# A hand-written operation order replaced by another in an attention-plus-MLP kernel, with fewer dummy matmuls and one more pre-summed batch

## The chip, the cores and the metric

The kernel runs on one core of one Trainium2 chip. The metric is the device time of one execution in microseconds (us), taken as the median over several executions. A difference of about 1% is what a measurement of this kernel can tell from no change.

The engines are named as in the profile: PE is the matmul engine (PEld its weight loads), DVE the vector engine, ACT the scalar engine, POOL the engine that also issues the software-driven DMAs, SP the one that issues the other DMAs. Each engine runs its own instructions strictly in the order in which the program lists them, and semaphores make it wait for the other engines.

## The reference

There are 8 batches, 8 heads, 576 tokens, head size 64. 16 "beacon" keys and values stand ahead of the 576 ordinary ones and are always visible; the others are causal. The attention output, 4608 tokens by 512, goes through a two-layer MLP (512 to 2048 to 512) with an ELU between.

```python
scores = scale * np.matmul(q, k_all.transpose(0, 1, 3, 2))   # k_all = beacon_k, k
scores = np.where(causal, -1000000000.0, scores)
a = np.exp(scores - scores.max(-1, keepdims=True))
a /= a.sum(-1, keepdims=True) + 1e-09
attn = np.matmul(a, v_all)
x = attn.transpose(0, 2, 1, 3).reshape(B * S, H * D)
h = x @ w_in
g = np.where(h > 0.0, h, np.exp(np.minimum(h, 0.0)) - 1.0)
out = g @ w_out
```

## The kernel before, in words

**An order written out by hand.** The kernel defines small steps, each a Python function of a few instructions, and then one long string (L790 to L912) lists 1501 words such as `S.3.3` or `lk.3.0`. A word is a step's name and its arguments. The helper `run` (L784) goes through the string and emits every step's instructions. So the string is at the same time the order of the instructions on each engine: PE takes its instructions from the words that have matmuls, POOL takes its own from the words that issue its DMAs, and so on. No engine overtakes within its own list.

**Attention.** Scores are made transposed, keys on partitions. Heads go in pairs p = 0 to 3. For one pair and batch the causal blocks (five key chunks j) lie behind one another as 1664 columns. From batch 1 on, the 4 x 1664 columns of a batch are cut into 13 groups of 512: `S.b.g` (L309) makes group g on PE, `x.b.g` (L330) takes the exponential on ACT, `m` (L347) masks the diagonal blocks on DVE. So group 3 holds the end of pair 0 and the start of pair 1. `L.b.g` (L402; here g is a half of the heads, pairs 2g and 2g+1) makes the row sums on PE with a matrix of ones, `n` the reciprocals on ACT, `W.b.g` (L449) the product with V, and `M.b.g` (L479) scales the result into the MLP's input. Batch 0 has a finer cut of its own.

**How q and k arrive.** Batches 0 to 2 are loaded by POOL (`lq`, L247), transposed on PE (`T`, L255) and copied to `qks` by DVE or ACT (`cq`, `ck`). Batches 3 to 7 go another way. `lk.b.n` (L758) is a POOL DMA that converts all of q (n = 0) or k (n = 1) of batch b to bf16 in DRAM, as `scr`. `lt.b.x` (L763) issues two transposing DMAs on SP, first q and then k, for the pairs 2x and 2x+1; each reads the whole half of `scr`, so `lt.b.x` needs both `lk.b.0` and `lk.b.1`, whichever x it is. They write `stq[b % 2][x]`, the staging buffer that batch b-2 used. `lp.b.x` (L773) is a small POOL step that puts the beacon keys and zeros into the same buffer; it must wait until the transposes or score matmuls of batch b-2 have read the columns that it overwrites. `lv` (L780) loads V; two V buffers go round.

**Pre-summed batches.** For batches 3 to 7, the steps `D.b.p.n` (L387) add the five key chunks of a pair's exponentials on DVE into the free buffer `qks`, and `L` then needs one pass of ones over the sum in place of one pass for each chunk.

**The MLP.** `F` (L503) is the first layer on PE, `e`, `u`, `k` or `e`, `r`, `g` the ELU on ACT and DVE (the second form puts one ACT step onto DVE). `G`, `o`, `s` are the second layer for the first token tiles. From tile 2 on, `Q` (L618) and `J` (L632) make the second layer with seven products in place of eight, from sums prepared by `Z`, `wt`; tiles 8 and 9 do the same for the first layer (`P`, `K`, `X`, `H`, `E`, `U`, `V`). A trailing `.v` on `J`, `U`, `K` puts a copy or a relu on DVE in place of ACT.

**Dummy matmuls.** `warm.4` (L204) is four matmuls of 512 columns, `wm.4` (L211) four of 128 columns, on zeros, into a bank that nobody reads. Before: three `warm.4` and eighteen `wm.4`, all ahead of the first `F`.

```python
            if b >= BD:                                   # L418, BD = 3
                for i in range(4):
                    nc.tensor.matmul(out=r_[32 * i:32 * (i + 1), QA:S], lhsT=ones, rhs=presum[b, 2 * g + i // 2] ...
            else:
                quad(b, g, QA, S, r_[:, QA:S], None, True)
        for n_ in range(2):                               # L766, lt
            nc.sync.dma_start_transpose(out=t[:, :, n_, NB:SK], in_=scr[b, n_] ...
```

Of the kernel before, what the change touches and what calls it, by code (L numbers as in the profile page):

```python
# [17 lines left out]
def kernel(  # L18
# [12 lines left out]
    P = 128  # L31

    B, H, S, D = q.shape
# [44 lines left out]
    BD = 3  # L78
# [305 lines left out]
    presum = {}  # L384
# [17 lines left out]
    def L(b, g):  # L402
# [388 lines left out]
    warm.4 warm.4 lq.0.0.0.4 lq.0.1.0.4 lv.0.2 warm.4 wm.4 ident T.0.0.0 bt ck.0.0.0 wm.4  # L791
    T.0.1.0 bk cb.0.2 cb.0.0 wm.4 lq.0.0.4.8 S.0.0.0 x.0.0.0 lq.0.1.4.8 T.0.0.1 lq.1.0.0.4 tri
    cq.0.1.0 cb.0.1 S.0.1.0 x.0.1.0 lv.0.0.1 T.0.1.1 wm.4 cq.0.0.1 S.0.0.2 x.0.0.2 S.0.0.1 wm.4
    cq.0.1.1 T.0.3.0 cb.0.3 x.0.0.1 cq.0.3.0 m.0.0.2 S.0.1.3 x.0.1.3 T.0.2.0 cq.0.2.0 S.0.1.1
    wm.4 x.0.1.1 T.0.2.1 S.0.3.0 wm.4 wm.4 x.0.3.0 T.0.3.1 cq.0.2.1 cq.0.3.1 S.0.2.0 wi.0
    S.0.2.3 x.0.2.0 wm.4 wm.4 x.0.2.3 wm.4 wm.4 m.0.0.0 m.0.2.0 m.0.1.0 S.0.3.1 x.0.3.1 wm.4
    S.0.1.2 x.0.1.2 m.0.3.0 cb.1.3 L.0.A S.0.0.3 S.0.2.1 x.0.0.3 x.0.2.1 wm.4 S.0.3.2 x.0.3.2
    T.1.0.0 n.0.A T.1.1.0 wm.4 wm.4 W.0.A.0 cb.1.0 cq.1.0.0 m.0.2.3 S.1.1 m.0.1.3 m.0.1.2
    m.0.3.2 cb.1.1 ck.1.1.0 x.1.1 wm.4 wm.4 S.1.2 W.0.A.1 x.1.2 S.0.3.3 x.0.3.3 S.0.2.2 m.0.0.3
    x.0.2.2 M.0.A.0 M.0.A.1 F.0.2 e.0.2 u.0.2 k.0.2 lv.0.3.4 S.1.5 x.1.5 m.0.2.2 S.1.0 F.0.1  # L800
    x.1.0 F.0.0 m.0.3.3 e.0.1 u.0.1 k.0.1 L.0.B n.0.B W.0.B.1 M.0.B.1 F.0.3 e.0.0 e.0.3 u.0.0
    u.0.3 W.0.B.0 S.1.4 x.1.4 wi.1 F.0.4 M.0.B.0 k.0.3 F.1.1 lq.1.0.4.8 e.0.4 u.0.4 e.1.1 k.0.0
    r.1.1 S.1.3 cb.1.2 x.1.3 g.1.1 F.0.5 T.1.3.0 cq.1.3.0 e.0.5 u.0.5 T.1.2.0 ck.1.2.0 k.0.5
    F.1.7 e.1.7 r.1.7 g.1.7 S.1.6 x.1.6 F.1.4 e.1.4 r.1.4 g.1.4 S.1.11 S.1.7 x.1.11 F.0.6 x.1.7
    S.1.8 F.1.5 k.0.4 H.1.0 e.0.6 r.0.6 x.1.8 wo.0 lq.2.0.4.8 g.0.6 G.0.1.0 e.1.5 r.1.5 g.1.5
    S.1.12 x.1.12 lq.2.0.0.4 wo.1 S.1.9 x.1.9 F.1.2 lv.1.0.1 S.1.10 x.1.10 F.1.3 m.1.2.1 cb.2.1
    wo.2 e.1.3 T.2.2.0 u.1.3 cq.2.2.0 T.2.1.0 ck.2.1.0 G.0.0.0 e.1.2 u.1.2 T.2.0.0 lv.1.2.3.4
    ck.2.0.0 lv.2.2.3.4 T.2.3.0 k.1.3 wo.3 cq.2.3.0 F.0.7 G.0.0.1 cb.2.0 e.0.7 m.1.0.0 m.1.2.0
    S.2.1 x.2.1 wt.1.0 S.2.0 m.1.1.0 G.0.1.1 F.1.0 m.1.0.1 S.2.3 lp.4.0 x.2.0 m.1.1.1 m.2.0.0
    m.1.3.1 u.0.7 L.1.0 m.1.3.0 e.1.0 r.1.0 g.1.0 x.2.3 F.1.6 n.1.0 M.1.0.0 k.0.7 L.1.1 H.1.2  # L810
    n.1.1 G.0.1.2 lk.3.0 e.1.6 u.1.6 M.1.1.0 lv.2.0.1 k.1.2 W.1.0 M.1.0.1 W.1.1 S.2.2 M.1.1.1
    x.2.2 F.2.6 cb.2.2 e.2.6 S.2.4 H.2.2 S.2.5 x.2.5 F.2.11 u.2.6 m.2.0.1 e.2.11 u.2.11 lk.3.1
    G.0.0.2 k.2.11 k.1.6 k.2.6 cb.2.3 G.0.0.3 x.2.4 F.2.8 lt.3.0 e.2.8 F.2.14 u.2.8 o.0.0 s.0.0
    S.2.8 wt.1.1 wt.2.0 e.2.14 u.2.14 S.2.12 x.2.8 k.2.14 wt.2.1 F.2.15 k.2.8 F.2.0 e.2.15
    u.2.15 G.1.1.0 e.2.0 x.2.12 G.1.1.1 r.2.0 k.2.15 g.2.0 S.2.6 x.2.6 F.2.9 G.1.1.2 S.2.11
    S.2.7 F.2.1 e.2.9 x.2.11 x.2.7 r.2.9 m.2.3.1 g.2.9 G.0.1.3 e.2.1 u.2.1 S.2.9 S.2.10 x.2.10
    F.2.2 m.2.1.0 lp.3.0 e.2.2 F.2.13 x.2.9 m.2.1.1 G.1.1.3 o.1.1 e.2.13 L.2.0 m.2.2.1 u.2.2
    r.2.13 g.2.13 S.3.3 G.1.0.0 n.2.0 M.2.0.0 x.3.3 o.0.1 F.2.3 e.2.3 u.2.3 F.2.4 S.3.1 x.3.1
    k.2.2 k.2.1 H.1.1 W.2.0 wt.4.0 M.2.0.1 e.2.4 u.2.4 m.2.3.0 lt.3.1 lp.3.1 m.2.2.0 S.3.4 s.0.1
    x.3.4 F.2.10 F.2.12 k.2.4 S.3.8 L.2.1 k.2.3 e.2.10 u.2.10 e.2.12 r.2.12 x.3.8 G.1.0.1 g.2.12  # L820
    n.2.1 k.2.10 F.2.5 e.2.5 M.2.1.0 u.2.5 F.2.7 S.3.2 x.3.2 e.2.7 W.2.1 M.2.1.1 S.3.6 Q.2.0.7
    F.3.5 wt.3.0 x.3.6 H.4.2 S.3.9 S.3.0 u.2.7 Z.2.3.0 k.2.7 Q.2.7.14 e.3.5 u.3.5 x.3.9 x.3.0
    k.2.5 Z.2.1.0 Z.2.3.1 Z.2.1.1 F.3.2 e.3.2 Z.2.2.0 F.3.8 S.3.11 e.3.8 u.3.2 k.3.2 m.3.0.0
    S.3.5 x.3.5 G.1.0.2 G.1.0.3 F.3.1 o.1.0 x.3.11 S.3.12 wt.4.1 m.3.1.0 u.3.8 S.3.10 m.3.1.1
    Q.2.14.21 e.3.1 u.3.1 k.3.1 lk.4.1 x.3.12 F.3.0 Z.2.2.1 k.3.5 m.3.0.1 J.2.0 e.3.0 Q.2.21.28
    lk.4.0 lt.4.0 D.3.0.0 D.3.1.0 u.3.0 k.3.0 D.3.1.1 s.1.0 D.3.1.2 Q.2.28.35 J.2.1 k.3.8 F.3.14
    S.4.1 x.3.10 lk.5.0 lp.4.1 Z.2.4.0 e.3.14 u.3.14 k.3.14 S.4.0 x.4.0 D.3.0.1 x.4.1 Q.2.35.42
    F.3.4 Q.2.42.49 D.3.0.2 e.3.4 u.3.4 Z.2.4.1 D.3.1.3 J.2.2.v F.3.9 e.3.9 u.3.9 Q.2.49.56
    k.3.4 S.4.4 lp.5.0 x.4.4 lv.3.0.1 S.3.7 F.3.6 k.3.9 Q.2.56.63 D.3.0.3 e.3.6 u.3.6 x.3.7
    lk.5.1 m.3.3.1 F.3.15 e.3.15 u.3.15 F.3.3 S.4.3 lv.3.2.3.4 W.3.0 lt.4.1 x.4.3 H.2.0 e.3.3  # L830
    u.3.3 m.3.2.0 lt.5.0 H.4.0 wt.3.1 k.3.15 m.3.3.0 k.3.6 L.3.0 Q.2.63.70 Q.2.70.77 k.3.3 J.2.3
    n.3.0 D.3.2.0 F.3.11 e.3.11 D.3.3.0 M.3.0.1 F.3.12 D.3.3.1 M.3.0.0 m.3.2.1 Q.2.77.84 u.3.11
    D.3.3.2 e.3.12 u.3.12 D.3.2.1 D.3.2.2 lp.5.1 Z.3.3.0 F.3.7 e.3.7 u.3.7 D.3.3.3 Q.2.84.91
    D.3.2.3 S.4.11 x.4.11 S.4.12 x.4.12 k.3.7 J.2.4 F.3.10 e.3.10 k.3.11 r.3.10 g.3.10 F.3.13
    L.3.1 n.3.1 M.3.1.0 W.3.1 Q.2.91.98 M.3.1.1 lt.5.1 k.3.12 Z.3.1.0 e.3.13 u.3.13 J.2.5 k.3.13
    m.4.3.1 F.4.8 e.4.8 S.4.10 x.4.10 S.4.2 F.4.3 x.4.2 e.4.3 u.4.8 Q.2.98.105 Q.2.105.112
    m.4.0.1 u.4.3 J.2.6.v S.4.6 S.4.5 Z.3.3.1 m.4.1.0 Q.3.0.7 x.4.5 k.4.3 x.4.6 F.4.7 e.4.7
    Q.3.7.14 u.4.7 m.4.0.0 F.4.6 S.5.4 e.4.6 u.4.6 m.4.1.1 x.5.4 S.4.7 k.4.8 Q.3.14.21 Z.3.1.1
# [102 lines left out]
```

## Time and profile before

| what | us |
|---|---|
| median of three executions | 335.81 |
| lowest, highest | 334.82, 337.05 |
| the profiled execution, device time | 336.74 |
| its span (first to last instruction) | 335.0 |
| PE busy in the span | 325.6 |
| DVE, ACT, POOL busy | 284.7, 278.1, 90.9 |

The span is 1.7 us shorter than the device time of the same execution. Busy shares are averages over the whole span; which engine a stage hangs on is read from the stage itself. A matmul row in a timeline gives the start and the modelled end; two rows behind one another overlap by some 0.1 us, so the time that a step costs PE is the distance from its start to the next start.

### The profile page before, as it was taken

The page shows a single profiled execution, that of the slowest core. Times are in us where ns is not written, and L with a number is a line of the kernel's source. Part 1 is how long each engine was busy: PE and PEld are TensorE (multiplying, and loading weights), DVE is VectorE, ACT ScalarE, POOL GpSimd, SP SyncE. Part 2 cuts the span into 40 slices and gives each one's busy share as a digit, 9 for nine tenths or more (in the row PEclk, how much of TensorE's full clock was granted, in tenths as well). Part 3 has the DMA queues.
Part 4 walks back from the last instruction along what each step waited for, and adds up shares of the span by engine and source line. Part 5 has one row for each costly group of instructions (what it writes and reads, how often), then busy time and mean ns, then how long its engine had stood idle before and what let it go on. Part 6 is the DMA issues. An engine that isn't in the chain of part 4 may idle for free.

```text
span 335.0 us, 8848 instructions
## 1 busy us (share of the span) xinstructions
PE 325.6 (97%) x3616; PEld 210.7 (63%) x3616; DVE 284.7 (85%) x601; ACT 278.1 (83%) x452; POOL 90.9 (27%) x117
## 2 busy tenths in 40 slices
PE   8899999999999999999999999999999999999994
PEld 3566766544455565656566656655666888788783
DVE  3555788875979999999899989998999999999982
ACT  2689999799999988999997998988987586889610
POOL 8968268630017284440061050000000000000000
PEclk9989999999999999999999999999999999999999
DMA  9999999999909999999199094320110110111112
GB/s 115 157 179 175 205 189 163 158 154 162 163 3 102 172 140 173 166 178 118 53 136 151 5 68 102 71 35 31 38 61 31 45 54 31 48 47 33 64 65 95
DMA packets 129113, 34.66 MB, mean 103 GB/s; under 512 B 112944, under 2 KB 127536, under 8 KB 129072
## 3 DMA queue, kind: packets, MB, share of 16 engines
q0 software_dynamic: 94944, 18.49, 68.8%
q1 hardware_dynamic: 33408, 15.34, 22.8%
q8 instruction: 28, 0.46, 0.6%
q10 hardware_dynamic: 720, 0.26, 0.3%
q14 instruction: 13, 0.11, 0.1%
HBM read 37.22 MB, written 15.34 MB: 157 GB/s over the span
## 4 chain that ended last, share of the span: by engine, by line
PE 87%; DVE 3%; ACT 3%; POOL 2%; DMA 2%; issue 1%; ACTq 0%; DVEq 0%; POOLq 0%
PE hps L512 30%; PE ops L627 29%; PE sc L321 8%; PE ut L378 6%; PE hps L697 5%; PE ops L563 4%; PE lt L378 2%; DMA kst<-in_k_dram 2%; ACT et L336 2%; POOL qst L136 1%; PE lt L420 1%; PE w L214 1%; PE tp L267 1%; PE ub L378 1%; DVE gt L554 1%
## 5 line engine op out<-in xcount | busy, mean ns | idle before, releaser
L512 PE MATMUL hps<-xT,w_in 128*128 128x512 f16 (+1 forms) x544 | 118.5, 354 | 0.3
L336 ACT ACTIVATE et<-sc 128x1024 f16<-128x1024 f32 (+2 forms) x114 | 105.7, 978 | 10.1 <-PE sc L321 9.5
L627 PEld LDWEIGHTS <-gt 128*128 128x128 f16 x768 | 73.3, 98 | 20.2 <-issue 3.7
L522 ACT ACTIVATE e<-hps 128x512 f32<-128x512 f32 x120 | 73.5, 620 | 13.8 <-PE hps L512 11.2
L512 PEld LDWEIGHTS <-w_in 128*128 128x128 f16 x544 | 50.6, 98 | 41.4 <-issue 4.4
L537 DVE SCALAR_TENSOR_TENSOR gt<-e,r 128x512 f16<-128x512 f32 x100 | 67.0, 684 | 8.0 <-ACT r L527 7.9
L527 ACT ACTIVATE r<-hps 128x512 f16<-128x512 f32 x100 | 61.9, 626 | 0.0
L627 PE MATMUL ops<-w_out,gt 128*128 128x256 f16 x384 | 50.7, 273 | 0.4 <-DVE gt L537 0.4
L627 PE MATMUL ops<-wt,gt 128*128 128x256 f16 x384 | 50.7, 273 | 0.0
L149 POOL DMA_DIRECT2D v<-in_v_dram x40 | 34.7, 919 | 5.0 <-DMA w_out<-in_moe_w_out_dram 2.7
L341 DVE TENSOR_TENSOR et<-et,triu 128x512 f16<-128x512 f16 (+4 forms) x108 | 31.2, 332 | 2.6 <-ACT et L336 2.4
L584 DVE TENSOR_TENSOR gt<-gt 128x1024 f16<-128x1024 f16 x48 | 32.4, 685 | 0.5
L378 PEld LDWEIGHTS <-v 128*32 128x32 f16 (+1 forms) x800 | 17.1, 96 | 10.6 <-issue 3.1
L394 DVE TENSOR_TENSOR qk<-qk,et 128x672 f16<-128x672 f16 (+2 forms) x60 | 21.2, 368 | 0.4
L378 PE MATMUL ut<-et,v 128*32 128x464 f16 (+3 forms) x560 | 20.9, 296 | 0.0
L472 DVE TENSOR_TENSOR xT<-ut,rl 128x672 f16<-128x672 f32 (+12 forms) x26 | 16.4, 670 | 3.1 <-PE ut L378 2.1
L643 DVE TENSOR_TENSOR osb<-ops,sm 128x512 f32<-128x512 f32 x24 | 16.4, 683 | 2.0 <-PE ops L627 1.9
L627 PE MATMUL ops<-w_out,s 128*128 128x256 f16 x128 | 17.1, 273 | 0.0
L563 PE MATMUL ops<-w_out,gt 128*128 128x512 f16 x64 | 16.0, 380 | 0.0
L736 DVE SCALAR_TENSOR_TENSOR gt<-e,r 128x512 f16<-128x512 f32 x24 | 15.9, 684 | 0.1
L627 PEld LDWEIGHTS <-s 128*128 128x128 f16 x128 | 12.3, 98 | 3.1 <-issue 0.3
L554 DVE TENSOR_TENSOR gt<-hps,r 128x512 f16<-128x512 f32 x20 | 13.7, 687 | 0.7
(111 smaller groups left out, 408.1 us busy)
## 6 DMA issues: line engine op xcount, KB each, us to landing
out_dram<-osb SPq DMA_DIRECT2D x35, 256.0 KB, 2.3
v<-in_v_dram POOLq DMA_DIRECT2D x24, 128.0 KB, 8.1
scr<-in_q_dram POOLq DMA_DIRECT2D x5, 576.0 KB, 15.6
scr<-in_k_dram POOLq DMA_DIRECT2D x5, 576.0 KB, 14.1
w_in<-in_moe_w_in_dram POOLq DMA_DIRECT2D x16, 128.0 KB, 5.9
w_out<-in_moe_w_out_dram POOLq DMA_DIRECT2D x4, 512.0 KB, 10.1
qst<-in_q_dram POOLq DMA_DIRECT2D x4, 288.0 KB, 8.7
kst<-in_k_dram POOLq DMA_DIRECT2D x4, 288.0 KB, 9.4
```

The costliest lines, as they stand in the source:

```text
L149: nc.gpsimd.dma_start(out=vt[b][r0:r0 + n, j, :, :], in_=v[b, :, ilo[j]:ilo[j] + n, :].rearrange("h s d -> s h d"),)
L321: nc.tensor.matmul(out=s[:, h, a - c0:e - c0], lhsT=t[D * h:D * (h + 1), 1, P * j:P * (j + 1)], rhs=t[D * h:D * (h + 1), 0, NB + qa + a - ...
L336: nc.scalar.activation(out=ets[b, d][:, :, a - EC2 * d:e - EC2 * d], in_=sc[b, g][:, :, a - c0:e - c0], func=AFT.Exp, bias=0.0, scale=SCALE)
L341: nc.vector.tensor_tensor(out=o, in0=o, in1=i, op=ALU.mult)
L378: nc.tensor.matmul(out=t[32 * i:32 * (i + 1), a - qa:e - qa], lhsT=ones[0:kc[j], :] if half is None else v16[0:kc[j], j, h, 32 * half:32 * ...
L512: nc.tensor.matmul(out=h[:, n_, :], lhsT=w_in16[:, cc, P * fc:P * (fc + 1)], rhs=xt[k][:, cc, a - TT * k:e - TT * k], start=(cc == 0), sto ...
L522: nc.scalar.activation(out=eb[t, i], in_=flat(hp[t, i]), func=AFT.Exp, bias=0.0, scale=1.0)
L527: nc.scalar.activation(out=rb[t, i], in_=flat(hp[t, i]), func=AFT.Relu, bias=0.0, scale=1.0)
L537: nc.vector.scalar_tensor_tensor(out=half(t, i), in0=eb[t, i], scalar=1.0, in1=rb[t, i], op0=ALU.subtract, op1=ALU.min)
L563: nc.tensor.matmul(out=ob[t, tb_], lhsT=gt[:, fc, P * tb_:P * (tb_ + 1)], rhs=w_out16[:, fc, :], start=(fc == 0), stop=(fc == NFC - 1))
L584: (nc.vector if eng == "v" else nc.gpsimd).tensor_tensor(out=o_, in0=a_, in1=b_, op=op_)
L627: nc.tensor.matmul(out=xy[t, n_][:, qd, :], lhsT=lw[:, P * qd:P * (qd + 1)], rhs=wt_[:, c, :], start=(first and qd == 0 and c == 0), stop= ...
```

## The change

Three things change; every other function stays as it is.

First, the condition in `L` is now whether a sum exists, `(b, 2 * g) in presum`, in place of `b >= BD`. Second, the string has ten `wm.4` fewer (eight are left) and eight new words `D.2.0.0` to `D.2.1.3`, so that `L.2.0` takes the pre-summed form; `L.2.1` keeps the old one. Third, the words are in another order throughout. Some choices of engine change with it: eighteen words carried `.v`, now fourteen do, and twenty ELU blocks used the DVE form, now nineteen do. In all ACT has 457 instructions for 452, DVE 597 for 594, PE 3560 matmuls for 3616; POOL and SP have the same ones in another order.

The POOL queue, from the string (each word is one to eight DMAs, or a few short POOL instructions):

- before: lq.0.0.0.4, lq.0.1.0.4, lv.0.2, ident, lq.0.0.4.8, lq.0.1.4.8, lq.1.0.0.4, tri, lv.0.0.1, wi.0, lv.0.3.4, wi.1, lq.1.0.4.8, wo.0, lq.2.0.4.8, lq.2.0.0.4, wo.1, lv.1.0.1, wo.2, lv.1.2.3.4, lv.2.2.3.4, wo.3, lp.4.0, **lk.3.0**, lv.2.0.1, **lk.3.1**, lp.3.0, lp.3.1, lk.4.1, lk.4.0, lk.5.0, lp.4.1, lp.5.0, lv.3.0.1, lk.5.1, lv.3.2.3.4, lp.5.1, lv.5, lk.6.0, lk.6.1, lv.4, ...
- after: lq.0.0.0.4, ident, lq.0.1.0.4, lq.0.0.4.8, tri, lq.0.1.4.8, lv.0.2, lv.0.0.1, lq.1.0.0.4, wi.0, lv.0.3.4, wi.1, lq.1.0.4.8, wo.0, wo.1, lp.3.0, lq.2.0.4.8, lq.2.0.0.4, wo.2, lv.1.0.1, lv.2.2.3.4, lp.4.0, lv.2.0.1, lv.1.2.3.4, lp.4.1, wo.3, **lk.3.1**, lp.3.1, **lk.3.0**, lv.3.0.1, lk.5.1, lk.7.0, lk.4.0, lk.4.1, lk.7.1, lv.3.2.3.4, lk.5.0, lk.6.1, lp.6.0, lk.6.0, lp.5.0, lp.5.1, lp.6.1, lv.4, ...

The SP queue at its start:

- before: **lt.3.0**, s.0.0, **lt.3.1**, s.0.1, lt.4.0, s.1.0, J.2.1, lt.4.1, lt.5.0, ...
- after: **lt.3.1**, **lt.3.0**, s.0.1, lt.4.0, s.1.0, J.2.1, lt.4.1, s.0.0, J.2.4, lt.5.0, ...

PE's order around the first use of batch 3 (`S.3.3`):

- before: ..., F.2.2, F.2.13, G.1.1.3, L.2.0, **S.3.3**, G.1.0.0, F.2.3, F.2.4, S.3.1, W.2.0, S.3.4, F.2.10, F.2.12, S.3.8, ...
- after: ..., F.2.2, F.2.13, L.2.0, **S.3.3**, G.0.1.3, F.2.3, G.1.0.0, F.2.4, S.3.1, W.2.0, S.3.4, F.2.12, F.2.10, G.1.0.1, S.3.8, ...

The matmul words ahead of the first `F` (F.0.2) are the same in both, apart from `wm.4`. The diff, cut:

```diff
-            if b >= BD:
+            if (b, 2 * g) in presum:
...
-    warm.4 warm.4 lq.0.0.0.4 lq.0.1.0.4 lv.0.2 warm.4 wm.4 ident T.0.0.0 bt ck.0.0.0 wm.4
-    T.0.1.0 bk cb.0.2 cb.0.0 wm.4 lq.0.0.4.8 S.0.0.0 x.0.0.0 lq.0.1.4.8 T.0.0.1 lq.1.0.0.4 tri
...
-    S.0.2.3 x.0.2.0 wm.4 wm.4 x.0.2.3 wm.4 wm.4 m.0.0.0 m.0.2.0 m.0.1.0 S.0.3.1 x.0.3.1 wm.4
...
-    n.1.1 G.0.1.2 lk.3.0 e.1.6 u.1.6 M.1.1.0 lv.2.0.1 k.1.2 W.1.0 M.1.0.1 W.1.1 S.2.2 M.1.1.1
...
-    G.0.0.2 k.2.11 k.1.6 k.2.6 cb.2.3 G.0.0.3 x.2.4 F.2.8 lt.3.0 e.2.8 F.2.14 u.2.8 o.0.0 s.0.0
...
+    lq.0.0.0.4 warm.4 warm.4 warm.4 ident bt wm.4 wm.4 T.0.1.0 wm.4 bk T.0.0.0 lq.0.1.0.4 cb.0.0
+    ck.0.1.0 cb.0.1 S.0.1.0 cq.0.0.0 S.0.0.0 lq.0.0.4.8 tri T.0.0.1 T.0.1.1 cq.0.0.1 cq.0.1.1
...
+    cb.2.2 g.0.6 x.1.8 e.1.5 r.1.5 g.1.5 cb.2.0 G.0.1.0 lp.3.0 S.1.12 x.1.12 k.0.4 S.1.9 x.1.9
...
+    u.2.11 m.2.1.0 lp.4.1 wo.3 G.0.0.2 G.0.0.3 x.2.5 F.2.8 D.2.0.0 e.2.8 F.2.14 u.2.8 H.2.2
...
+    D.2.0.1 k.2.14 D.2.0.2 e.2.15 F.2.9 u.2.15 k.2.8 G.1.1.0 D.2.1.0 S.2.8 m.2.1.1 D.2.1.1
+    lk.3.1 G.1.1.1 x.2.8 e.2.9 F.2.0 u.2.9 S.2.11 D.2.1.2 e.2.0 r.2.0 g.2.0 D.2.1.3 S.2.7
+    G.1.1.2 D.2.0.3 F.2.1 G.1.1.3 x.2.11 k.2.9 x.2.7 S.2.10 e.2.1 u.2.1 S.2.9 x.2.9 x.2.10 F.2.2
+    lp.3.1 wt.4.0 e.2.2 u.2.2 k.2.15 lk.3.0 lt.3.1 F.2.13 lt.3.0 o.1.1 e.2.13 L.2.0 S.3.3
+    G.0.1.3 n.2.0 m.2.2.0 m.2.3.0 m.2.2.1 r.2.13 g.2.13 o.0.1 F.2.3 e.2.3 M.2.0.0 k.2.1 r.2.3
...
```

## The prediction

> **What bounds the kernel now.** I read the page first, its busy line and its slices:
>
> ```profile
> PE 325.6 (97%) x3616; PEld 210.7 (63%) x3616; DVE 284.7 (85%) x601; ACT 278.1 (83%) x452; POOL 90.9 (27%) x117
> ...
> PEclk9989999999999999999999999999999999999999
> DMA  9999999999909999999199094320110110111112
> ```
>
> PE looks like the bound, the DMA engines are full for the first quarter, and in the third slice the PE clock drops. Next, the busy time by stretches, cut at the drop and where the first `F` begins:
>
> ```profile
> core 0: us, PE busy (x) PEld busy (x) DVE busy (x) ACT busy (x) POOL busy (x), PEclk, DMA share, GB/s
> 0.00:16.30 16.30, 13.26 (x180) 7.64 (x180) 6.90 (x20) 7.50 (x9) 14.58 (x28) 1.00 1.18 135
> 16.30:19.70 3.40, 3.40 (x41) 2.55 (x36) 3.03 (x15) 1.82 (x4) 1.33 (x3) 0.50 1.66 187
> 19.70:28.00 8.30, 7.20 (x183) 5.11 (x181) 4.17 (x13) 8.26 (x11) 7.02 (x12) 1.00 1.26 173
> 28.00:330.60 302.60, 301.75 (x3222) 195.38 (x3220) 270.13 (x553) 260.17 (x430) 67.95 (x76) 1.00 0.90 99
> ```
>
> From 28.0 to 330.6 us PE is busy for 301.75 of 302.60 us. Starts in its timeline are spaced alike for like work (0.22 us for a 512-column `F` matmul, 0.11 for a 256-column `Q`); I find six longer gaps in the whole stretch, 1.4 us together. So no order can gain much there, and any wait put in front of PE is paid in full. Before 28 us, ACT's timeline shows who waits:
>
> ```profile
> 8.70 4.95 ACT L336 ACTIVATE et<-sc 128x832 f16<-128x832 f32 x6 [1.13 <-PE sc L321]
> 15.49 0.86 ACT L336 ACTIVATE et<-sc 128x832 f16<-128x832 f32 x1 [1.84 <-PE sc L321]
> 16.91 1.62 ACT L336 ACTIVATE et<-sc 128x832 f16<-128x832 f32 x2 [0.55 <-PE sc L321]
> 19.55 3.89 ACT L336 ACTIVATE et<-sc 128x832 f16<-128x832 f32 x5 [1.02 <-PE sc L321]
> ```
>
> There 1.84 + 0.55 + 1.02 = 3.4 us of the exponentials' chain are lost. Last, the resource that the new order disturbs most, the transposing loads of batch 3 on SP, and PE where batch 3 is first used (the row at 83.67 is `S.3.3`):
>
> ```profile
> 62.73 7.82 SPq L767 DMA_TRANSPOSE qst<-scr  x2
> 71.71 0.38 SPq L576 DMA_DIRECT2D out_dram<-osb  x1
> 72.26 7.45 SPq L767 DMA_TRANSPOSE kst<-scr  x2
> 86.27 0.36 SPq L576 DMA_DIRECT2D out_dram<-osb  x1
> 86.84 2.74 SPq L767 DMA_TRANSPOSE qst<-scr  x2
> ```
>
> ```profile
> 82.74 0.90 PE L378 MATMUL lt<-et,ones 128*32 128x464 f16 x24
> 83.46 0.27 PE L378 MATMUL lt<-et,v 128*32 128x112 f16 x8
> 83.67 0.40 PE L321 MATMUL sc<-qst 64*128 64x48 bf16 x6
> ```
>
> The DMA view, asked for each issue alone, gives the landings. The four transposes of batch 3 start at 62.73, 69.17, 72.26 and 75.42 and land after 8.4, 7.8, 9.6 and 10.6 us: at 71.1, 77.0, 81.9 and 86.0. lt.4.0, issued at 86.84 and 88.33 as the DMA load ends, lands after 4.0 and 3.9 us, at 90.8 and 92.2. lk.3.0 lands at 62.6, lk.3.1 at 69.1. So lt.3.0 was ready 6.7 us ahead of `S.3.3`, and lt.3.1 12 us ahead of its first user at 98.4.
>
> **The change part by part.** The sum goes against the profiled execution, 336.74 us (span 335.0 and 1.7 around it), 0.9 above the median.
>
> *Dummies.* Forty fewer. At 17.16 to 18.98 sixteen of them took 1.82 us of PE, with S.0.3.1 queued behind; ACT's wait of 1.02 us ended with it. The rest stand in gaps where PE waits anyway, and cost nothing.
>
> *Start.* `F.0.2` started at 27.88, right after S.0.2.2, whose bank an exponential had to free. The same sixteen S groups, S.1.1, S.1.2 and their ACT work precede it in both orders. I lose 0.5 us at the first exponential (bk's transposes and two wm.4 now precede T.0.1.0), gain about 1.0 of the 1.84 (the loads behind T.0.2.1 have lv.0.2, 144 KB, no longer ahead of them; its two DMAs land 0.8 us apart, and its issue took 1.5) and, of the other waits, the 0.55 and the 1.02 plus 0.5 elsewhere: 2.6 us earlier. Bound on the gain: `F.0.2` needs wi.0, as deep in the POOL queue as before; its last DMA, issued at 19.81, lands after 4.9 us at 24.8, so at most 3.0. Bound on the loss: the clock row; a window at 0.50 of 3.4 us costs 1.7 us, so -1.0 to +3.0.
>
> *Pre-sum of batch 2.* L.2.0 went from 82.74 to 83.67, 0.93 us; batch 3's summed ones take 0.45. Gain 0.5. On DVE it adds 2 x (634 + 500 + 369 + 234) ns = 3.5 us of adds between 66 and 84 us, where DVE is busy 12.0 of 18.0 us; hidden. D.2.1.0 must wait for S.2.6 (its buffer), which moves 4 us forward for that; the ELU of F.2.0 queues behind it. Without that room L.2.0 would start late by up to 3.5 us.
>
> *Engine choices.* ACT gets 5 instructions more, about 3 us (0.6 each), DVE 3 more with the eight adds in it. Over 300 us this lies beside PE.
>
> *POOL order, up to V.* lp.3.0 now stands ahead of the four loads of batch 2 and must wait for the q part of T.1.2.0 (PE at 40.2, less 2.6), so these issue at 38 in place of 29.7. The queue hides most: their old landings, 40.5 to 44.9, were set by the DMAs ahead, and wo.1 (2.6 us per 512 KB between landings) now fills that time. They land near 44 to 48.4, T.2.1.0 wants the last at 48. lv.1.2.3.4 now follows lv.2 (five V loads, 0.8 us each) and lp.4.0; it lands at 54.1 + 3.7 + 1 to 2 for gaps, 59 to 60.5; W.1.0 uses it from 59.4 on. I take 1.0 us of PE waits for both; bounds 0 and 3.
>
> *lk.3 and lt.3.* Both lk.3 are issued after wo.3, lk.3.1 first. The bytes ahead of the second are the same as before and the DMA engines are full, so the second one lands at about 70: the old 69.1 and 1 for gaps (bounds 67.8, the sum of landing distances since lq.1.0.4.8 with no gap, and 72). Any lt.3 needs both, so the first transpose starts at 70, not 62.7. And SP issues lt.3.1 first, while `S.3.3` needs lt.3.0: four transposes stand ahead of `S.3.3` after 70, where one stood after 69.1. POOL's next words (lv.3.0.1, lk.5.1, lk.7.0, lk.4.0, lk.4.1, lk.7.1; three such lk kept the engines full from 62 to 87) load the same engines throughout. Under that load the first took 8.4 us and the next landings followed by 5.8, 4.9 and 4.1 us; other loaded pairs (lt.5.0, lt.6.0) by 3.4. So the fourth lands at 70 + 8.4 + 3 x 3.4 to 5.0 = 88.6 to 93.4; I take 91, nearest to batch 3's own rows. Unloaded, by lt.4.0: 70 + 4.0 + 3 x 1.35 = 78.
>
> The copies beside them suffer alike: lk.4.0, with two transposes beside it, landed 9.9 us after lk.4.1, where lk.3.0 needed 3.8 after wo.3.
>
> PE reaches `S.3.3` at 83.67 - 2.6 - 0.5 (L.2.0) - 0.8 (G.0.1.3 moved behind it) - 0.4 (two gaps that may close) + 1.0 = 80.4. It then stands until 91: 10.6 us. Everything on PE is queued behind it. Such a stand is three times the 3.4 us of the slow clock row; I add one window at half clock, 1.7.
>
> *Sum.* 336.7 - 2.6 - 0.5 - 0.4 + 1.0 + 10.6 + 1.7 = 346.5. From the other end: 91 + (336.74 - 83.67) + 0.8 + 1.7 = 346.6. Against the median 0.9 less: 345.7.
>
> *After that.* With PE some 10 us later, the DMAs of later batches have that much more room. lv.4 waits for lp.6.1 and so S.4.9, 12 us ahead of W.4.0; V loads of that size took 9.3 us (lv.7). lt.5.1 is issued behind J.3.1, about 12 us ahead of S.5.6; loaded pairs took 10 to 13. 0 to 2 us, taken as 0.
>
> **Rivals.** *The transposes keep pace (ends on the other side).* If lt.3's four transposes run as lt.4.0's did, they are through at 78, and `S.3.3` doesn't wait. The point is the landing of the fourth: below 80.4 the change is no slower. Then 336.7 - 2.6 - 0.5 - 0.4 + 1.0 = 334.2, 333.3 against the median. For it: lt.4.0's rows. Against it: those ran as the queue emptied; here it is full. The skill's same page, "Latency and other measured facts", gives a transposing DMA 261 GB/s; at 295 KB each, four would take 4.5 us (an estimate by that page), which would be this rival. The loaded rows here contradict it.
>
> *A short stand.* The second lk lands at 67.8 and the first transpose takes 7.1 us, as lt.5.0's did, the others 3.4 each: 67.8 + 7.1 + 10.2 = 85.1. A stand of 4.7 us, with half the clock loss: 334.2 + 4.7 + 0.8 - 0.9 = 338.8.
>
> *The start fails.* With few dummies the clock could be at 0.50 for two windows before 28 us, which costs up to 3.4 us of PE time and eats the 2.6. Without the stand this is 336.7, or 335.8 against the median, no change; with the stand nothing is altered, since the transposes then set the time. For it: the one window before came after only 3 us of thin work. Against it: real matmuls take the dummies' place earlier. The skill's page "TensorE: Matmul & The Clock Gate", Part 4, has it that PE transposes don't count as activity for the clock; by that rule this rival is the likelier start, since 144 of them stand there.
>
> **How the numbers follow.** Stand of 7 us or more: 0.58, likeliest, 345.7 (342 to 349). Short stand: 0.16, 337 to 342. No stand: 0.14 with the start gained (332.5 to 334.5), 0.12 with it lost or with small waits elsewhere (334.5 to 337). 1% is about what a measurement of this kernel can tell from no change: 332.5 to 339.2. Slower by over 1%: 0.58 + 0.10 = 0.68; faster by over 1% only if the start gives its whole 3.0 and no early wait comes, 0.08; within, 0.24. The range, 334 to 349, leaves out the best starts and the slowest transposes.
>
> **What would show it.** Right: a row `sc<-qst` at S.3.3 with PE idle some 10 us before it, released by a DMA `qst<-scr`; the SP rows begin near 70 with kst; the clock at 0.50 for one window there; the first `F` near 25.3; L.2.0's matmuls on `qk`. Wrong: the transposes of kst starting before 66, or four of them landing within 10 us; then the time is below 337.

## The result

The kernel after takes 347.35 us (median of 4 runs, 345.09 to 348.12), the kernel before 336.43 us (4 runs, 334.82 to 337.72). The ratio is 1.0316, with a 95% interval from 1.0244 to 1.0388: slower. The prediction was 345.7 us. The profiled execution took 348.12 us, its span is 346.3.

Three lines of the page, the busy line and two of the slices of 8.7 us:

```profile
PE 326.8 (94%) x3560; PEld 209.3 (60%) x3560; DVE 287.7 (83%) x604; ACT 281.9 (81%) x457; POOL 89.1 (26%) x117
...
PE   7899999994599999999999999999999999999995
...
PEclk9679999999599999999999999999999999999999
```

PE is busy for only 1.2 us more than before, but the span is 11.3 us longer, so 10.1 us of it is idle time, and the 4 and the 5 in the tenth and eleventh slices say where. The clock row has a 5 beside them that was not there before, and it is lower in slices two and three. The group of costliest instructions that holds `S.3.3` has the whole idle time in its last column:

```profile
L321 PE MATMUL sc<-qst 64*128 64x80 bf16 (+13 forms) x160 | 12.4, 255 | 9.4 <-DMA qst<-scr 9.4
```

PE's timeline at that place, to be set beside the one of before (start, length, then in brackets the idle time and what ended it):

```profile
80.89 0.38 PE L420 MATMUL lt<-qk,ones 128*32 128x464 f16 x4
81.10 0.22 PE L378 MATMUL lt<-et,ones 128*32 128x112 f16 x4
81.15 0.27 PE L378 MATMUL lt<-et,v 128*32 128x112 f16 x8
90.79 0.61 PE L321 MATMUL sc<-qst 64*128 64x48 bf16 x6 [9.37 <-DMA qst<-scr]
91.33 1.89 PE L563 MATMUL ops<-w_out,gt 128*128 128x512 f16 x4
...
101.37 1.03 PE L563 MATMUL ops<-w_out,gt 128*128 128x512 f16 x4
```

`L.2.0` now begins with four matmuls on `qk`, the pre-sum, and `S.3.3` waits 9.37 us for a transposing load. Behind it four matmuls of 128x512 take 1.89 us, where the same row at 101.37 takes 1.03: that is the half clock. SP's queue in its timeline:

```profile
72.68 5.68 SPq L767 DMA_TRANSPOSE kst<-scr  x2
78.48 6.69 SPq L767 DMA_TRANSPOSE qst<-scr  x2
```

It begins ten microseconds later than before, and with kst (lt.3.1). The landings, from the DMA view: lk.3.1 at 68.24, lk.3.0 at 72.53, then the four transposes at 80.55, 84.01, 87.24 and 90.75. `S.3.3` starts 0.04 us after the last.

The same stretches as before (busy time per engine, then granted clock, DMA share, GB/s):

```profile
16.30:19.70 3.40, 3.11 (x42) 1.83 (x42) 2.07 (x13) 3.29 (x5) 1.07 (x2) 0.50 1.21 197
19.70:28.00 8.30, 7.27 (x172) 5.21 (x164) 4.31 (x13) 7.85 (x11) 6.34 (x11) 0.88 1.27 174
28.00:80.00 52.00, 51.49 (x725) 30.67 (x720) 39.73 (x85) 49.06 (x76) 32.38 (x40) 1.00 1.70 162
80.00:100.00 20.00, 10.63 (x93) 4.16 (x92) 7.27 (x16) 7.34 (x13) 7.83 (x6) 0.74 2.04 165
100.00:341.00 241.00, 240.25 (x2374) 159.28 (x2372) 225.96 (x458) 206.06 (x346) 26.80 (x32) 1.00 0.52 75
```

From 28 to 80 and from 100 to 341 us PE is as full as before. Nearly all that is lost lies between 80 and 100. Against before, `F.0.2` starts 1.2 us earlier (26.68), PE is free for `S.3.3` 2.25 us earlier (81.42) and starts it 7.1 us later.

### The profile page after: what moved, and what is told of

Its sections match the earlier page's. It is cut to its first block, busy times and chain, and to the rows that moved or that the text cites. A ratio compares the mean times of both kernels' runs of the same rounds, so it can differ in the third digit from the quotient of the medians.

```text
span 346.3 us, 8728 instructions
## 1 busy us (share of the span) xinstructions
PE 326.8 (94%) x3560; PEld 209.3 (60%) x3560; DVE 287.7 (83%) x604; ACT 281.9 (81%) x457; POOL 89.1 (26%) x117
## 4 chain that ended last, share of the span: by engine, by line
PE 78%; DVE 8%; ACT 6%; DMA 4%; issue 2%; SPq 1%; ACTq 0%; DVEq 0%
PE hps L512 27%; PE ops L627 24%; PE sc L321 8%; PE ut L378 5%; PE ops L563 4%; PE hps L697 4%; DMA qst<-scr 3%; ACT et L336 2%; PE lt L378 2%; DVE gt L537 1%; ACT e L719 1%; DMA lo<-in_beacon_k_dram 1%; SPq L767 1%; PE tq L267 1%; DVE qk L394 1%
## 5 line engine op out<-in xcount | busy, mean ns | idle before, releaser
L512 PE MATMUL hps<-xT,w_in 128*128 128x512 f16 (+1 forms) x544 | 120.6, 357 | 0.8 <-ACT r L527 0.4
L537 DVE SCALAR_TENSOR_TENSOR gt<-e,r 128x512 f16<-128x512 f32 x101 | 68.3, 684 | 9.8 <-ACT r L527 9.4
L527 ACT ACTIVATE r<-hps 128x512 f16<-128x512 f32 x101 | 62.6, 626 | 0.0
L394 DVE TENSOR_TENSOR qk<-qk,et 128x672 f16<-128x672 f16 (+2 forms) x66 | 23.4, 367 | 0.5
L321 PE MATMUL sc<-qst 64*128 64x80 bf16 (+13 forms) x160 | 12.4, 255 | 9.4 <-DMA qst<-scr 9.4
L563 PE MATMUL ops<-w_out,gt 128*128 128x512 f16 x64 | 17.9, 412 | 0.0
L736 DVE SCALAR_TENSOR_TENSOR gt<-e,r 128x512 f16<-128x512 f32 x24 | 16.1, 683 | 0.1
L760 POOL DMA_DIRECT2D scr<-in_k_dram x5 | 11.1, 2215 | 14.7 <-issue 14.7
```

Of the source, the lines that this page charges most:

```text
L321: nc.tensor.matmul(out=s[:, h, a - c0:e - c0], lhsT=t[D * h:D * (h + 1), 1, P * j:P * (j + 1)], rhs=t[D * h:D * (h + 1), 0, NB + qa + a - ...
L512: nc.tensor.matmul(out=h[:, n_, :], lhsT=w_in16[:, cc, P * fc:P * (fc + 1)], rhs=xt[k][:, cc, a - TT * k:e - TT * k], start=(cc == 0), sto ...
L527: nc.scalar.activation(out=rb[t, i], in_=flat(hp[t, i]), func=AFT.Relu, bias=0.0, scale=1.0)
L537: nc.vector.scalar_tensor_tensor(out=half(t, i), in0=eb[t, i], scalar=1.0, in1=rb[t, i], op0=ALU.subtract, op1=ALU.min)
L563: nc.tensor.matmul(out=ob[t, tb_], lhsT=gt[:, fc, P * tb_:P * (tb_ + 1)], rhs=w_out16[:, fc, :], start=(fc == 0), stop=(fc == NFC - 1))
```

## The experiments

The theory: the end is late by the stand at `S.3.3` and the half clock behind it, and the stand has three parts, the late second lk.3, lt.3.1 ahead of lt.3.0, and POOL's copies beside the transposes. The rivals: the transposes are slow by themselves, or the new order loses time elsewhere too. All times are medians. Ratios, with 95% intervals, are to the kernel before on the same chip (334.89 to 335.31 us beside the experiments). They are not quotients of the medians (335.93 by 334.89 would be 1.0031 for e1), and the experiments ran on several chips, so small differences between rows of the table say little.

| kernel | us | ratio |
|---|---|---|
| after | 347.35 | 1.0316 (1.0244 to 1.0388) |
| after, old POOL order and lt.3.0 first (e1) | 335.93 | 1.0009 (0.9978 to 1.0039) |
| after, old POOL order only (e5) | 339.56 | 1.0104 (1.0041 to 1.0167) |
| after, lt.3.0 first only (e6) | 337.35 | 1.0049 (1.0017 to 1.0082) |
| after, other transfers held back (e7) | 342.85 | 1.0207 (1.0143 to 1.0270) |
| the same, lk.4 first behind it (e9) | 337.29 | 1.0034 (0.9995 to 1.0074) |
| after, PE kept busy in the stand (e8) | 345.65 | 1.0290 (1.0224 to 1.0357) |
| before with the new POOL order up to lk.3 and lt.3.1 first (e11) | 345.69 | 1.0299 (1.0250 to 1.0348) |
| before, ten wm.4 fewer (e2) | 334.94 | 0.9985 (0.9960 to 1.0011) |
| e1 with ten wm.4 more (e3) | 335.94 | 1.0004 (0.9974 to 1.0034) |
| e1 without the pre-sum (e4) | 335.48 | 0.9997 (0.9968 to 1.0027) |
| e3 without the pre-sum (e10) | 335.09 | 0.9981 (0.9952 to 1.0010) |
| e3 with the last two words changed over (e12) | 335.80 | 1.0004 (0.9979 to 1.0030) |

**e1: the fault taken out.** Words of POOL and SP only; the words between them stand as they were.

```diff
-    wo.1 lp.3.0 lq.2.0.4.8 lq.2.0.0.4 wo.2 lv.1.0.1 lv.2.2.3.4 lp.4.0
-    lv.2.0.1 lv.1.2.3.4 lp.4.1 wo.3 lk.3.1 lp.3.1 lk.3.0
+    lq.2.0.4.8 lq.2.0.0.4 wo.1 lv.1.0.1 wo.2 lv.1.2.3.4 lv.2.2.3.4 wo.3
+    lp.4.0 lk.3.0 lv.2.0.1 lk.3.1 lp.3.0 lp.3.1 lp.4.1
...
-    lt.3.1 F.2.13 lt.3.0
+    lt.3.0 F.2.13 lt.3.1
```

> The kernel after, with the POOL words from wo.1 to lp.4.1 put back into the order of the kernel before, and lt.3.0 ahead of lt.3.1 again; the new order of everything else, the fewer dummies and the pre-sum of batch 2 stay. Theory (the whole loss is the wait for lk.3 and lt.3 and the clock behind it): the second lk lands near 68.5 us, lt.3.0 has landed before TensorE comes to S.3.3 near 80.5, no stand, no half clock near 90, and what is left of the change is a gain: 1.2 us at F.0.2 and 0.4 us in L.2.0, so about 334.7 us where the kernel before has 336.4 (333.5 to 336). Rival (the new order costs time elsewhere too, after S.3.3 or in the start): 338 us or more.

The stand is gone and so is the clock drop at 90 us. PE's timeline of e1 at `S.3.3`:

```profile
81.12 0.27 PE L378 MATMUL lt<-et,v 128*32 128x112 f16 x8
81.33 0.40 PE L321 MATMUL sc<-qst 64*128 64x48 bf16 x6
```

The second lk.3 landed at 68.33, lt.3.0 at 71.35 and 76.62, 4.7 us ahead of PE. The 335.93 us is at the top of the theory's range: all of the loss comes back, but the gain of 1.6 us that should be left over doesn't show. e2 to e4, e10 and e12 look for it.

**e11: the fault alone, put into the kernel before.** The same words the other way round, with lt.3.1 straight ahead of lt.3.0; everything else is the kernel before.

```diff
-    lt.3.0
+    lt.3.1 lt.3.0
...
-    lt.3.1
```

> The kernel before with the suspected fault alone: POOL's words from wo.1 to lp.4.1 in the order of the kernel after (lk.3.1 and lk.3.0 last), and lt.3.1 straight ahead of lt.3.0; all else as before, dummies, start and row sums too. Theory (this and nothing else makes the kernel after slower): the second lk lands near 72 us, lt.3.0's second transpose near 90, TensorE stands some 7 to 9 us at S.3.3 (it comes there 0.5 us later than in the kernel after, with L.2.0 at full length), then one to three windows at half clock: 344 to 347.5 us. Rival (the new order of the other engines has a part in the stand): below 341 us.

PE's timeline of e11 at `S.3.3`:

```profile
83.27 0.27 PE L378 MATMUL lt<-et,v 128*32 128x112 f16 x8
90.67 0.61 PE L321 MATMUL sc<-qst 64*128 64x48 bf16 x6 [7.13 <-DMA qst<-scr]
```

As the theory has it: second lk at 71.83, last transpose at 90.62, 345.69 us. The sum closes. `S.3.3` is 7.0 us later than in the profiled execution of before, and 3.4 us of work behind it ran at half clock, 1.7 us; the span grew by 8.8 (343.8 to 335.0). Together with e1 this shows both ways that POOL's order up to lk.3 and the order of the two lt.3 make the loss. Which of POOL's words between wo.1 and lp.4.1 make the second lk late wasn't split further.

**e5 and e6: one half of the repair each.** e5 has e1's POOL order and lt.3.1 still first; e6 has the new POOL order and only this:

```diff
-    lt.3.1 F.2.13 lt.3.0
+    lt.3.0 F.2.13 lt.3.1
```

> The kernel after with only the POOL words from wo.1 to lp.4.1 put back into the order of the kernel before; lt.3.1 stays ahead of lt.3.0. Theory (the stand is the late second lk plus four transposes one after the other under load, 18.07 us from issue of the first to landing of the last in the kernel after): the second lk lands near 68.5 us, the last transpose near 86.8, TensorE comes to S.3.3 near 81 and stands some 5.8 us; the end some 4 to 5 us before the kernel after, near 342.5 us. Rival 1 (the order of lt.3.0 and lt.3.1 is all): a stand of 9 us as after, 347. Rival 2 (the lateness of the lk is all): no stand, 335.

> The kernel after with only lt.3.0 ahead of lt.3.1 again; the new POOL order stays. Theory (the two transposes that S.3.3 needs then land where lt.3.1's landed, 80.55 and 84.01 us): a stand of 2.6 us at S.3.3, which TensorE reaches at 81.4, so some 6.7 us less than after, and most of the 3 us that the half clock cost is gone too: 338 to 340.5 us. Rival (the lateness of the lk is all, and the load on the queues makes either order late): the stand stays above 6 us, 344 or more.

e5 stood less than I expected. Its PE timeline:

```profile
81.00 0.27 PE L378 MATMUL lt<-et,v 128*32 128x112 f16 x8
83.56 0.40 PE L321 MATMUL sc<-qst 64*128 64x48 bf16 x6 [2.28 <-DMA qst<-scr]
```

The reason is in the landings. A word lt issues the q half first, and that needs only lk.3.0. With lk.3.0 ahead of lk.3.1 again, the first transpose starts at 62.90, six microseconds before lk.3.1 has landed (68.89), and only three are left behind it; the fourth lands at 83.51, not at 86.8. I had counted both lk.3 as the condition of any transpose. The 2.28 us then cost 3.9: the profiled runs are 340.56 and 336.64 us, `S.3.3` is 2.2 us later than in e1, and a window from 84.6 to 88.1 us at half clock is 1.7.

The profiled execution of e6 took 342.01 us, far above its median, and PE was two microseconds late from 40 us on. Its landings are 82.38 and 85.81 for lt.3.0, 7.86 and 11.29 us after its first issue, as lt.3.1's in the kernel after (7.87 and 11.33). Its stand at `S.3.3` is the one that the theory had, with one window at half clock behind it (87.2 to 90.6 us):

```profile
85.86 0.40 PE L321 MATMUL sc<-qst 64*128 64x48 bf16 x6 [2.61 <-DMA qst<-scr]
```

The median of 337.35 is below the theory's 338 to 340.5; how long the stand was in the other nine executions isn't known. Each half of the repair alone takes most of the loss away, because in e1 lt.3.0 is 4.7 us early. The order of lt alone costs 6.9 us of landing (76.62 to 83.51) and both together 14.1 (to 90.75), and PE notices only what goes beyond 4.7: 2.2 and 9.4, where 2.28 and 9.37 were measured.

**e7: the other transfers held back.** POOL may go on only when lt.3.0 has landed, so nothing of POOL's stands beside the transposes.

```diff
+    @step
+    def hold(b, x_):
+        t = stq[b % 2][x_][:, 0:2 * QW].rearrange("p (y i s) -> p y i s", y=2, i=2)
+        for n_ in range(2):
+            nc.gpsimd.tensor_copy(out=gt_, in_=t[:, :, n_, NB:2 * NB])
...
-    lt.3.0
+    lt.3.0 hold.3.0
```

> The kernel after with a step behind lt.3.0 in which POOL reads what lt.3.0 wrote (two copies of 128 by 8 elements), so that POOL sends lv.3.0.1, lk.5.1, lk.7.0, lk.4.0 and what follows only after the four transposes have landed; the order is kept. It takes the other transfers away from beside the transposes. Theory (load: the transposes that landed 3.5 to 6.7 us apart did so because POOL's copies shared the DMA engines): the last of the four lands near 81 us, a stand under 1 us at S.3.3, 335.5 to 337.5 us. Rival (a transpose takes that long by itself, one after the other): the last lands near 90, the stand stays near 9 us, 346 to 349 us. In between, the share of each can be read from the landings.

SP's queue in the timeline of e7:

```profile
72.59 3.06 SPq L767 DMA_TRANSPOSE kst<-scr  x2
75.77 3.05 SPq L767 DMA_TRANSPOSE qst<-scr  x2
...
101.40 5.54 SPq L767 DMA_TRANSPOSE qst<-scr  x2
```

The same four transposes, the first of them issued at the same time as in the kernel after (72.59 and 72.68), landed at 76.65, 78.17, 79.80 and 80.85 us: 4.0 us each from issue, 1.4 apart, where beside POOL's copies it was 7.9 to 9.6 and 3.4 apart. That is the load, shown. It is the condition of the stand and not what the change brought: in the kernel before the four ran under load too, 7.8 to 10.6 us each. `S.3.3` didn't wait (81.22). The time didn't follow, since the hold made lk.4 late, and lt.4.0 with it (the third row, with a landing at 114.35). PE's timeline of e7 there:

```profile
114.40 1.04 PE L321 MATMUL sc<-qst 64*128 64x64 bf16 x6 [6.44 <-DMA qst<-scr]
```

The stand had moved to batch 4, with its own half clock (0.50 from 110 to 120 us).

The Trainium skill, "DMA: Bandwidth & Descriptors", "Queues, rings and completion order", says that each DMA engine takes turns between the queues it has work for, a packet at a time; these landings agree with that. Its figure of 261 GB/s for a transposing DMA with a non-contiguous middle dimension ("Latency and other measured facts"), which a rival of the prediction uses, isn't reached here: 295 KB in 1.4 us are 211 GB/s, and in the kernel after 87. But the 211 is no limit of the DMA engines: SP's issues in e7 (72.59, 74.11, 75.77, 77.05) were as far apart as the landings.

**e9: the hold without its price.** As e7, with batch 4's loads first among those held.

```diff
-    lv.3.0.1 lk.5.1 lk.7.0 lk.4.0 lk.4.1
+    lk.4.0 lk.4.1 lv.3.0.1 lk.5.1 lk.7.0
```

> As the run that held POOL's transfers back behind the four transposes, with lk.4.0 and lk.4.1 first among those held (ahead of lv.3.0.1, lk.5.1, lk.7.0). In that run the last transpose landed at 80.85 us and S.3.3 did not wait, but lk.4 came late and TensorE stood 6.4 us at S.4.3 instead. Theory (the transposes are slow only beside POOL's copies, and the new stand is the queue position of lk.4): the four land about 4 us after issue, no stand at S.3.3, lk.4.1 lands near 97, lt.4.0 near 103, no stand at batch 4: 335.5 to 337.5 us. Rival (what is held back must be paid later wherever it is put): a stand of over 3 us somewhere in batch 3 or 4, 339 us or more.

Four transposes at 77.08 to 81.30 us, no stand at `S.3.3`, lt.4.0 at 104.68, none at batch 4. What PE waits for now is 1.28 us for a V tile of batch 3 (lv.3.0.1 was put behind). 337.29 us, inside the theory's range; the twelve runs lie between 334.98 and 340.85. So at `S.3.3` the lateness of the second lk.3 (72.89) and the order of the lt were harmless as soon as nothing loaded the queues beside them.

**e8: PE kept busy through the stand.** 38 dummies in the tile that `S.3.3` then overwrites.

```diff
+        if (b, g) == (3, (3,)):
+            for _ in range(38):
+                nc.tensor.matmul(
+                    out=s[:, 0, :], lhsT=zero[:, 0:P], rhs=zero[:, :], start=True, stop=True, skip_group_check=True)
```

> The kernel after with 38 dummy matmuls of 128 by 512 on zeros ahead of S.3.3, written into the tile that S.3.3 fills afterwards, so that TensorE works through the stand (38 by some 0.215 us are 8.2 us of the 9.4). Theory (the idle stand halves the granted clock behind it from 86.5 to 96.75 us, 5.9 us of work at half speed, some 3 us): the clock stays at 1.0, S.3.3 still starts near 90.8, what follows it takes 3 us less, 344.5 us. Rival (the half clock has another cause, or nothing hangs on it): the clock drops all the same or the end stays near 347.3 us.

The busy times and the clock (the 0.50 and the 1.00) of the stretch behind the stand, first of the kernel after, then of e8:

```profile
86.50:96.75 10.25, 5.96 (x19) 2.13 (x20) 2.71 (x5) 1.51 (x2) 4.68 (x4) 0.50 2.21 158
```

```profile
86.50:96.75 10.25, 9.17 (x85) 4.01 (x84) 3.78 (x8) 3.38 (x5) 4.68 (x4) 1.00 2.25 148
```

`S.3.3` starts at 90.56 in place of 90.79, and what follows is 2.9 us shorter (spans 343.2 and 346.3). That is half of the 5.96 us that PE worked there at half clock in the kernel after. The medians point the same way (345.65 and 347.35), but the intervals of the two ratios overlap; the size rests on the two profiles.

The Trainium skill, "TensorE: Matmul & The Clock Gate", Part 1, has the clock halved after at least one idle window of some 3.4 us. The length of the windows agrees (three of 3.41 us here). The least idle time doesn't: in e5 2.28 us of idle PE were enough for one window, while no half clock followed the waits of 1.08 us in e8 and 1.28 us in e9.

**e2 and e3: the dummies.** e2 takes ten wm.4 out of the kernel before, e3 puts ten into e1, at like places between T.0.1.1 and x.1.1. One of the ten in e3:

```diff
-    S.0.0.1 x.0.0.1
+    S.0.0.1 wm.4 x.0.0.1
```

> The kernel before without ten of its eighteen groups of four dummies (those among the words from T.0.1.1 to S.1.1), nothing else changed. Theory (Dummies: they stand in waits of TensorE for the exps and the first quarters, so their removal is worth under 1 us): F.0.2, at 27.88 us before, starts between 27.0 and 28.4 us, the end within 1 us of the kernel before. Rival (clock: the dummies keep the granted clock at full speed, which after shows at half from 11.4 to 21.7 us, against one window before): two windows more at half, F.0.2 1 to 3 us later, the end 1 to 3 us later.

> The repaired kernel (the kernel after with the old POOL order and lt.3.0 first) with ten groups of four dummies put back among the words from T.0.1.1 to x.1.1, so eighteen as before. Theory A (the half clock of the start costs what the new order of the start would have gained: predicted 2.6 us, seen 1.2): the clock stays at 1.0 from 11.4 us on or loses one window at most, F.0.2 starts near 25.5 us against 26.7, the end is 1 us earlier than the repaired kernel without them. Theory B (TensorE waits for the exps there anyway): F.0.2 within 0.4 us of the repaired kernel's, the same end. Theory C (the dummies stand in the way): F.0.2 0.5 to 1.2 us later, the end as much later.

The start in four stretches of 3.4 us, first the kernel after, then e3:

```profile
8.00:11.40 3.40, 2.33 (x64) 1.62 (x64) 2.04 (x3) 2.12 (x4) 3.40 (x6) 1.00 1.44 160
11.40:14.80 3.40, 3.33 (x52) 1.99 (x48) 2.02 (x6) 3.27 (x4) 3.13 (x6) 0.50 1.89 125
14.80:18.20 3.40, 3.11 (x45) 1.97 (x40) 3.40 (x16) 2.94 (x4) 1.99 (x5) 0.50 1.24 174
18.20:21.60 3.40, 3.40 (x51) 2.35 (x50) 1.13 (x8) 2.87 (x5) 2.23 (x4) 0.50 1.14 206
```

```profile
8.00:11.40 3.40, 2.66 (x66) 1.78 (x64) 1.96 (x3) 2.13 (x3) 3.40 (x6) 1.00 1.31 142
11.40:14.80 3.40, 3.38 (x67) 2.35 (x67) 2.45 (x6) 3.30 (x5) 3.13 (x6) 1.00 1.90 132
14.80:18.20 3.40, 3.28 (x61) 2.38 (x59) 3.23 (x16) 3.10 (x5) 1.87 (x4) 1.00 1.30 180
18.20:21.60 3.40, 3.00 (x87) 2.31 (x88) 1.26 (x8) 3.40 (x5) 1.18 (x3) 1.00 1.14 206
```

In the start of the new order the dummies hold the clock. `F.0.2` started at 26.74 in e1 and at 25.53 in e3, theory A's number. The last matmul ended 0.95 us earlier (328.86 and 329.81), but the medians are the same. The half clock set in at 11.41 behind a stretch in which PE was busy for 2.33 of 3.40 us and idle for 1.07; in e3 it was busy for 2.66. Idle time alone doesn't decide it: in the same execution of the kernel after PE was idle for 1.66 of the 3.41 us up to 83.08, and the clock stayed at 1.00 until 86.50.

In e2 the kernel before lost nothing: neither theory's time for `F.0.2` came (26.02 us; I had said 27.0 or more), and the median is unchanged. Both profiles have one window at half clock here, 16.3 to 19.7 us in the kernel before and 15.1 to 18.6 in e2; before, the sixteen dummies at 17.16 stood in it, which may be why `F.0.2` was as late as 27.88 (27.69 in e11, with the same start and also one window). The timed runs say more of my base than the profile. The kernel before's 35 beside e1 to e4 lie between 334.10 and 338.34 us, and they go with the mean granted clock: 334.10 to 335.14 us at 0.996 and above, 335.94 to 337.54 at 0.991 to 0.995, 337.42 to 338.34 at 0.989 and below. The profiled 336.74 had 0.993 and belongs to the middle group; how early `F.0.2` starts in the first one, no profile shows.

**e4 and e10: without the pre-sum.** e4 from e1, e10 from e3.

```diff
-            if (b, 2 * g) in presum:
+            if b >= BD:
...
-    D.2.0.0 D.2.0.1 D.2.0.2 D.2.1.0 D.2.1.1 D.2.1.2 D.2.1.3 D.2.0.3
```

> The repaired kernel (the kernel after with the old POOL order and lt.3.0 first) without the pre-sum of batch 2: the eight words D.2 are gone and L.2.0 takes its row sums from all exp tiles, as before. Theory (0.4 us of TensorE in L.2.0, and the 3.5 us of VectorE are hidden): L.2.0 takes 0.93 us instead of 0.53 and the end is 0.4 to 0.5 us later than the repaired kernel's. Rival (VectorE's eight additions hold up something that TensorE waits for): the end is the same or 0.5 to 1.5 us earlier without them.

> The repaired kernel with ten groups of dummies put back and without the pre-sum of batch 2. The repaired kernel took 335.93 us, with the dummies 335.94, without the pre-sum 335.48, where the kernel before took 334.89. Theory (the pre-sum of batch 2 saves TensorE 0.46 us in L.2.0 as the trace shows and costs nothing): 336.4 us, 0.46 us more than with it. Rival (VectorE's additions cost more than that somewhere behind, as the 335.48 hints): 335.0 us or less, 0.5 to 1 us less than with it. Resolution is about 0.5 us.

In the traces the theory holds in part. Without the pre-sum `L.2.0` takes 0.93 us in place of 0.46 (from its start to the next start), and the last matmul ends 0.46 us (e4) and 0.39 us (e10) later. But `F.0.2` is also 0.26 and 0.14 us later in these two, and from the start of `S.3.3` to the end of the last matmul they need 248.22 us, where e1 needs 248.49 and e3 248.45. So about half of what the pre-sum saves is lost again behind it, and 0.2 us is left; where it is lost stays open, since no wait of PE is put down to the additions.

The times go the other way, 0.45 and 0.85 us less, as the rival said. The 0.45 lies within the spread of the runs; the 0.85 doesn't (334.69 to 335.43 in e10, 335.45 to 336.55 in e3), though the two ran on different chips. In the profiles, one for each, the last transfer to HBM differs. From issue to landing it took 2.79 and 3.04 us in e1 and e3, 1.75 and 1.76 in e4 and e10. That doesn't go with the pre-sum alone: the kernel after and e6 to e9 have it too, and their last transfers took 1.92 to 2.03. e12 tests the one cause that I could think of, the order of the last two:

```diff
-    J.9.5 Jh.9.0 Jh.9.1
+    J.9.5 Jh.9.1 Jh.9.0
```

> The repaired kernel with the ten groups of dummies put back (335.94 us) and the last two words changed over, Jh.9.1 ahead of Jh.9.0 as in the kernel before: VectorE's copy and ACT's transfer first, ScalarE's copy and SP's transfer last. In the profiled run of 335.94 the last transfer, on ACT's queue, landed 3.04 us after its issue, against 1.71 us of the last one (SP's) in the kernel before, and that ate the 1.8 us that TensorE ended earlier. Theory (the order of the last two transfers decides how long the last one takes): the last lands near 1.7 us after issue, 1 us less, 334.9 us. Rival (the length of the last transfer does not hang on the order): the end stays within 0.4 us of 335.9, or is 0.4 us later since VectorE's copy takes 0.42 us and ScalarE's 0.37 behind it.

The last transfer took 2.00 us then, but the last matmul ended 0.41 us later than in e3 (329.27 and 328.86; `F.0.2` was 0.38 later), and the median is where it was: the rival. Why a transfer near the end is now and then 1 us longer stays open. No version beats the kernel before by more than its interval; e10 comes nearest, at 0.9981 (0.9952 to 1.0010).

## Why the prediction was right, and where its sum was off

The mechanism and the place were right: *lk.3 and lt.3* set the time. Everything else together comes out at nothing that the times can tell (e1), as gains and losses that cancel. That 345.7 is so near to 347.35 is partly luck, since errors of about 1 us lie on both sides of the sum. Term by term, against the profiled execution:

- *The stand.* 10.6 us said, 9.37 measured. Its end was placed well (91 and 90.75) out of two errors that cancel. The second lk came at 72.53, not 70: behind wo.3 (64.45) the two lk.3 took 3.8 and 4.3 us, and the queue as a whole ran 2.5 us later than my count of its bytes. The four transposes took 18.1 us from first issue to last landing, not 21: their distances were 3.5, 3.2 and 3.5 us, the lower end of my 3.4 to 5.0. Its beginning was 1.0 us later (81.4 for 80.4).
- *"Any lt.3 needs both."* Wrong for the first transpose, which needs lk.3.0 alone: before, it was issued at 62.73 behind lk.3.0 (62.6), with lk.3.1 still to land at 69.1, and e5 shows the same. It did no harm here because lk.3.0 happened to be the one that came last.
- *The clock behind it.* 1.7 us said for one window; three came, one of them partly in the stand, 3.0 us (e8). The one row I had, a short window at the start, gave the price of a window and not their number.
- *Start.* 2.6 us earlier said, 1.2 measured. With the clock held it is 2.35 (25.53 in e3); the half clock from 11.4 to 21.7 us, which the rival "the start fails" named, took half of it back. Both numbers are against one profiled execution that had a window at half clock in its own start.
- *Dummies.* Said to cost nothing apart from the sixteen. That left out what they are for in the new order, the clock, though the medians of e1 and e3 don't show it. PE was busy for 3.1 to 3.4 of every 3.4 us there in the kernel after, and yet at half clock. The rule that the rival cites (the Trainium skill, "TensorE: Matmul & The Clock Gate", Part 4: transposes don't count) fits that row, but no run here separates the transposes from the short matmuls beside them.
- *POOL order, up to V.* 1.0 us of early waits said, none measured. T.2.0.0, L.1.0 and W.1.0 start at 51.50, 56.69 and 60.49 us in the kernel after and at 51.57, 56.76 and 60.55 in e1, which has the old POOL order. The sum for lv.1.2.3.4 gives 58.8 to 59.8, not 59 to 60.5; its last load landed at 61.16, and PE shows no wait for it.
- *Pre-sum.* 0.5 us said, 0.46 in `L.2.0` measured, 0.2 of it left at the last matmul, and not found in the times.
- *The rest of the order.* Behind `S.3.3` it was put at nothing. From its start to the end of the last matmul PE needs 246.92 us in the kernel before and 248.49 in e1; 0.87 of that is the group G.0.1.3 that was moved there, 0.7 us is lost (0.25 of it with the pre-sum).
- *The rival on the other side* asked that the transposes run at the unloaded pace. e7 shows that pace, 4.0 us and 1.4 apart, but only with POOL's copies out of the way. With the stand gone I had 333.3 us; e1 has 335.93. In the profiles `S.3.3` came 2.34 us earlier in e1 than before (81.33 and 83.67), 0.87 of it the moved group; 0.7 was lost behind it, and the last transfer took 1.1 us longer (2.79 and 1.71), so the spans are 334.8 and 335.0. Also, the execution that the gains were counted against belongs to the middle group of its kernel's times by its clock, some 2 us above the first.

## What to carry to other kernels

When a load that feeds the bounding engine is moved, look at its queue position, at the order of the halves its user needs, and at what the same DMA engines carry at that time: here each fault alone was partly hidden by 4.7 us of slack and cost 1.4 (e6) and 3.6 us (e5) against e1, and together they cost 11. A wait of the bounding engine can cost more than its length, when the clock drops behind it: 2.28 us became 3.9. Look at the granted clock of the base run before counting gains against it.

## What was not expected of the hardware

- A transposing load of 295 KB landed 4.0 us after issue and 1.4 us after the one ahead when alone, and 7.9 to 9.6 us and 3.4 us beside three copies of POOL's queue (e7 and the kernel after).
- 2.28 us of idle PE were enough to halve the clock for the next 3.4 us (e5), and a PE that was busy for 3.1 to 3.4 us of each window, with transposes and short matmuls, stayed at half for three windows behind a stretch with 2.33 us of work; with ten groups of four short dummies among them it was held at full speed (e3).
- The last transfer of 128 KB took 1.7 to 3.0 us in the profiled executions of versions with the same work at the end.
